# Channel attention and SwiGLU on one core: preparation of the next blocks spread over more steps, its quarter differences on GpSimd

## The chip, the core and the metric

The kernel runs on one core of one Trainium2 chip. A core has TensorE (PE in the profile; PEld is its weight load), VectorE (DVE), ScalarE (ACT), GpSimd (POOL) and SyncE (SP, which here only issues DMAs). Each engine takes its instructions strictly in the order in which the program writes them and waits, where needed, for semaphores of the others. The metric is device time in microseconds (us), lower is better.

## The reference, cut to what matters

```python
def _attn_ref(q, k, v, tau):                    # q, k, v: (2, 6016, 256) float32
    qn = q / (norm(q, axis=1) + 1e-06)
    kn = k / (norm(k, axis=1) + 1e-06)
    s = kn.transpose(0, 2, 1) @ qn / tau        # 256 x 256 per batch
    a = softmax(s)                              # rows
    return v @ a
def _moe_ref(x, w_gate, w_val, w_out, rms_g):   # x: (12032, 256), d_ff = 1536
    xn = x / sqrt(mean(x * x) + 1e-06) * rms_g
    g = xn @ w_gate
    return (silu(g) * (xn @ w_val)) @ w_out
```

## The kernel before, in words

Everything is written out by hand in one order; no scheduler moves anything. Each float32 operand of a matmul is split in a high and a low part (`hi`, `lo`), and each product is made of three matmuls: hi·hi, lo·hi, hi·lo. ScalarE makes the high part with a copy, GpSimd or VectorE subtracts it for the low part.

The tokens are 94 tiles of 128, in 24 blocks: j = 0 to 11 for the first batch, 12 to 23 for the second. A block has four tiles (512 tokens); the last of each batch, 11 and 23, has three (384). A block is worked in NF = 12 steps f, one slice of 128 hidden channels each. Blocks 0 and 1 (`emit_hidden`) use plain products, while the scores of the second batch are made beside block 0. From block 2 on (`j >= WINO`), `emit_step` makes a block's hidden slices with seven half-size products instead of eight, from sums and differences of the four quarters of x (two halves of the channels by two halves of the tokens), called `xp`, and of the weights, called `s`, which `build_s` makes during blocks 1 and 2.

A step from block 2 on has 33 matmuls: 21 for products (7 products of three; 256 columns each, 192 in a three-tile block) and 12 in `emit_out` for the output `po` (three for each tile). Three steps overlap: `now` starts products 5 and 1, `mid` (the step before) adds 3 and 6, `old` (two steps back) adds 7, 2 and 4 and is finished. The products of a step share the PSUM tile `pu`. On PE the order is 7, 2, 5, 1, 3, 6, 4, then the 12 `po`. Product 4 overwrites a half of `pu` that VectorE must have read before (L612, the sum `z = u + t`); so PE's product 4 of each step waits for L612 of that step. VectorE then does L613, and in odd steps L623 and L634 (the multiplication with the Silu of the even step). ScalarE does L619 (copy to `t`), in even steps L621 and L632 (Silu), L628 (the second copy to `t`, which frees the half that product 7 of the next step overwrites), and in odd steps L553 twice (`gh`). GpSimd subtracts L559 twice (`gl`) in odd steps; `emit_out` uses `gh` and `gl` of a step four steps later.

Between the steps stands the preparation of the next block n = j + 1 (`ready`, a table by step; `ready0`, `ready1` and `ready` before, by block). Its pieces are:

- `v_moves`: two 32x32-block transposes of v on VectorE (L366), and the DMA load of a later v. `v_splits`: two ScalarE copies (L349) and two GpSimd subtractions (L350).
- `x(h)`, h = 0 or 1 (two tiles each): 12 matmuls v @ a into the PSUM tile `px` (L386). Before the change all such tiles of later blocks share one bank, tag "m" of `ps_m`.
- `squares_of_x(h)`: ScalarE squares with sums (L402), then two short GpSimd instructions for the inverse root `rr` (L411, L415). `xn(h)`: ScalarE scales `px` by `rr` (L427) into `xn`, which frees `px`.
- `emit_xT_move`: two transposes on VectorE (L463), then 16 DMAs on SP's queue that put the 32x32 blocks in place (`xw` to `xnT`). `xw` and `xp` share one buffer ("moved"), `xn` and `xnT` another ("xn").
- `emit_xT_parts`: ScalarE scales `xnT` by `rms_g` (L485), VectorE makes the differences of quarters `xp` (L490: 512 columns, L495 twice: 256).
- `emit_xT_round(i)`: the hi and lo parts of the quarters and differences in two rounds: two ScalarE copies (L507), two GpSimd subtractions (L509).

`at(j, f, ...)` adds the softmax pieces of the second batch (blocks 4 to 10) and pieces of `build_s` (blocks 1 and 2) behind those of the table.

Of the kernel before, what the change touches and what calls it, by code (L numbers as in the profile page):

```python
# [19 lines left out]
def kernel(  # L20
# [356 lines left out]
    def emit_x(j, h):  # L377
# [3 lines left out]
        psum, tag = (ps_m, "m") if j else (ps_gv, "u")  # L381
# [93 lines left out]

    def emit_xT_parts(j):
# [17 lines left out]
        for o, i0, i1 in ((t2, b2, t1), (t4, a2, t2)):  # L494
            nc.vector.tensor_tensor(out=o, in0=i0, in1=i1, op=ALU.subtract)  # L495
# [96 lines left out]
    def emit_step(j=None, f=None):  # L592
# [31 lines left out]
        if mid:
# [93 lines left out]
    with tc.manual_schedule():  # L718
# [174 lines left out]
        at(6, 7, lambda: softmax_min(1, 1))
        at(7, 7, lambda: (softmax_exp(1, 0), softmax_exp(1, 1)))
        at(B1 - 2, 6, lambda: softmax_div(1, 0))
        at(B1 - 2, 7, lambda: softmax_div(1, 1))
# [5 lines left out]
        def v_moves(n):  # L902
            if n < NB:
                move_v(n, 0)
                move_v(n, 1)
                if 2 < n + 1 < NB:
                    load_v(n + 1)
# [104 lines left out]
```

## Time and profile before

| | us |
|---|---|
| median of 3 runs | 1446.26 (1443.45 to 1446.7) |
| profiled execution | 1446.6 |
| its span | 1444.8 |
| PE busy | 1341.9 (93%) |
| ACT / DVE / POOL busy | 815.9 / 737.9 / 611.5 |
| PE idle before product matmuls L585 with a `w` weight | 68.7 |
| mean granted TensorE clock, share of full | 0.963 |

The busy times say that PE is the engine that works nearly all the time and that each of the others is idle for over four tenths of the span. The time between the span and the device time of the same execution is 1.8 us. Where PE waits, the view of waits names the instruction that released it; the timeline shows what that instruction's engine did before.

### The profile page before, as it was taken

To read this page: it belongs to the slowest core of one execution; us is meant where nothing else is said; L and a number is where in the kernel's file an instruction comes from. 1 tells how busy PE (TensorE), PEld (TensorE's weight loads), DVE (VectorE), ACT (ScalarE), POOL (GpSimd) and SP (SyncE) were. 2 spreads that over 40 slices of the span, in tenths; PEclk is the share of its full clock that TensorE was granted. 3 is DMA by queue.
4 is the path that set the end of the run, shared out by engine and by line. 5 is a ranking of instruction groups with operands and counts; after the bars stand their busy time and mean duration, and the time that the engine had idled before them with its cause. 6 is when DMAs were issued, how large, how long until landed. Compare 5 with 4: busy or idle time off the path is not lost. (4 is left out here: it accounts for less than half of the span.)

```text
span 1444.8 us, 26231 instructions
## 1 busy us (share of the span) xinstructions
PE 1341.9 (93%) x10212; PEld 1295.8 (90%) x10212; DVE 737.9 (51%) x1163; ACT 815.9 (56%) x1727; POOL 611.5 (42%) x550
## 2 busy tenths in 40 slices
PE   7999998899998898999899999999999999999998
PEld 6877887898998898999899898998999999999998
DVE  4689655653544544543543544544544445444443
ACT  4556554565565556555555655565555556555654
POOL 2137444444434444444334444445344434434332
PEclk8999998999999999999999999999999999999999
DMA  8857220120210201101202201201201202101100
GB/s 244 307 177 212 66 44 9 37 44 2 45 38 8 45 15 32 41 12 34 41 9 37 41 23 23 45 12 35 45 7 38 44 4 42 41 1 31 27 16 12
DMA packets 147677, 71.71 MB, mean 50 GB/s; under 512 B 100704, under 2 KB 139104, under 8 KB 147552
## 3 DMA queue, kind: packets, MB, share of 16 engines
q1 hardware_dynamic: 147168, 68.99, 19.2%
q0 software_dynamic: 384, 1.05, 0.4%
q8 instruction: 80, 1.31, 0.4%
q14 instruction: 45, 0.37, 0.1%
HBM read 46.40 MB, written 12.32 MB: 41 GB/s over the span
## 5 line engine op out<-in xcount | busy, mean ns | idle before, releaser
L559 POOL TENSOR_TENSOR gl<-zg,gh 128x512 fp32r<-128x512 f32 (+1 forms) x262 | 328.3, 1275 | 529.9 <-ACT gh L553 334.6
L585 PE MATMUL pu<-xt,w 128*128 128x256 f32 (+1 forms) x2376 | 378.6, 286 | 68.7 <-DVE zg L612 62.7
L619 ACT ACTIVATE t<-pu 128x512 f32<-128x512 f32 (+1 forms) x264 | 155.7, 590 | 486.3 <-DVE zv L613 254.0
L696 PE MATMUL po<-w,gh 128*128 128x256 f32 x2256 | 424.8, 287 | 0.0
L585 PE MATMUL pu<-xt,s 128*128 128x256 f32 (+1 forms) x2376 | 415.2, 284 | 2.1 <-ACT t L628 1.9
L585 PEld LDWEIGHTS pu<-xt,w 128*128 128x128 f32 x2376 | 324.3, 192 | 77.4 <-DVE zg L612 67.3
L696 PEld LDWEIGHTS po<-w,gh 128*128 128x128 f32 x2256 | 359.6, 195 | 2.2 <-ACT gh L553 0.2
L585 PEld LDWEIGHTS pu<-xt,s 128*128 128x128 f32 x2376 | 343.9, 193 | 3.8 <-ACT t L628 3.8
L696 PE MATMUL po<-w,gl 128*128 128x256 f32 x1128 | 322.7, 286 | 0.1
L612 DVE TENSOR_TENSOR zv<-pu,t 128x512 f32<-128x512 f32 (+1 forms) x132 | 88.9, 673 | 361.9 <-issue 184.3
L696 PEld LDWEIGHTS po<-w,gl 128*128 128x128 f32 x1128 | 220.3, 195 | 0.3 <-DVE gl L559 0.3
L553 ACT ACTIVATE gh<-zg 128x512 fp32r<-128x512 f32 (+1 forms) x264 | 157.4, 619 | 25.1 <-DVE zg L623 22.3
L612 DVE TENSOR_TENSOR zg<-pu,t 128x512 f32<-128x512 f32 (+1 forms) x132 | 89.5, 678 | 134.0 <-PE pu L585 93.2
L623 DVE TENSOR_TENSOR zg<-zg,zv 128x768 f32<-128x768 f32 (+1 forms) x132 | 145.8, 1105 | 4.5
L585 PE MATMUL pq<-xt,w 128*128 128x256 f32 (+1 forms) x792 | 139.3, 285 | 0.0
L585 PEld LDWEIGHTS pq<-xt,w 128*128 128x128 f32 x792 | 115.4, 194 | 0.0
L621 ACT ACTIVATE zg<-zg 128x768 f32<-128x768 f32 (+1 forms) x132 | 108.5, 822 | 1.4 <-DVE zg L613 1.4
L174 PE MATMUL s<-raw 128*128 128x256 f32 x376 | 95.2, 412 | 11.3 <-DMA raw<-in_k_dram 11.3
L628 ACT ACTIVATE t<-pu 128x256 f32<-128x256 f32 (+1 forms) x264 | 99.1, 375 | 2.6 <-PE pu L585 0.7
L174 PEld LDWEIGHTS s<-raw 128*128 128x128 f32 x376 | 76.6, 208 | 25.8 <-issue 14.0
L386 PE MATMUL px<-a,vt 128*128 128x256 f32 x564 | 79.1, 290 | 11.9 <-ACT xn L427 11.9
L350 POOL TENSOR_TENSOR vt<-vw,vt 128x512 fp32r<-128x512 f32 (+1 forms) x48 | 64.0, 1353 | 59.7 <-ACT vt L349 59.7
(97 smaller groups left out, 1286.3 us busy)
## 6 DMA issues: line engine op xcount, KB each, us to landing
out_dram<-ob SPq DMA_DIRECT2D x88, 128.0 KB, 2.3
raw<-in_q_dram SPq DMA_DIRECT2D x20, 512.0 KB, 5.8
raw<-in_k_dram SPq DMA_DIRECT2D x20, 512.0 KB, 7.0
v<-in_v_dram SPq DMA_DIRECT2D x80, 128.0 KB, 3.8
xnT<-xw SPq DMA_DIRECT2D x320, 32.0 KB, 1.9
wraw<-in_moe_w_gate_dram SPq DMA_DIRECT2D x12, 256.0 KB, 3.6
wraw<-in_moe_w_val_dram SPq DMA_DIRECT2D x12, 256.0 KB, 4.1
wraw<-in_moe_w_out_dram SPq DMA_DIRECT2D x12, 256.0 KB, 4.7
```

What stands on the lines that cost most here:

```text
L174: nc.tensor.matmul(out=s_ps[b][:, c, :], lhsT=r[:, 1, t, c * P:(c + 1) * P], rhs=r[:, 0, t, :], start=(t0 + t == 0 and c == 0), stop=(t0 + ...
L350: engine.tensor_tensor(out=hl[1], in0=x, in1=f32(hl[0]), op=ALU.subtract)
L386: nc.tensor.matmul(out=px[:, i, :], lhsT=w[:, c, t * P:(t + 1) * P], rhs=x[:, c, :], start=(i == 0 and c == 0 and m == 0), stop=(c == KC - ...
L553: nc.scalar.activation(out=gh, in_=hh, func=AF.Copy)
L559: engine.tensor_tensor(out=gl, in0=hh, in1=f32(gh), op=ALU.subtract)
L585: nc.tensor.matmul(out=out, lhsT=wm[wi], rhs=xm[xi], start=(start and q == 0), stop=(q == 2), skip_group_check=True,)
L612: nc.vector.tensor_tensor(out=z[:, 1:], in0=u, in1=t[:, :2], op=ALU.add)
L619: nc.scalar.activation(out=nt[:, 1:], in_=nu, func=AF.Copy)
L621: nc.scalar.activation(out=zg[:, 1:], in_=zg[:, 1:], func=AF.Silu)
L623: nc.vector.tensor_tensor(out=zg[:, 1:], in0=zg[:, 1:], in1=z, op=ALU.mult)
L628: nc.scalar.activation(out=mt[:, 0], in_=mu[:, 1], func=AF.Copy)
L696: nc.tensor.matmul(out=o_ps[j][t // 2][:, t % 2, :], lhsT=g[:, t * P:(t + 1) * P], rhs=wo[w][:, f, :], start=(first and t % 2 == 0 and m = ...
```

## The change

Seven edits, all in the order of the work and in who does it. The differences of quarters go from VectorE to GpSimd. The scaling by `rms_g` gets a step of its own (`emit_xT_scale`) ahead of them. The second half of `px` and of `pxt` goes to another PSUM bank (`ps_s`) for blocks from 2 on. In `emit_step`, L628 now stands ahead of the Silu (even steps) and of the product of gate and value (odd steps). The table `ready` is written anew: x of a block is made five steps sooner, in the block before the previous one (`then(2, ...)` means block j + 2), with the pieces that depend on each other mostly in different steps; block 2 gets a table of its own. The softmax pieces move to even steps. Two tests `if n < NB` move into `then`.

```diff
-        psum, tag = (ps_m, "m") if j else (ps_gv, "u")
+        psum, tag = (ps_s, "s") if j >= WINO and h else (ps_m, "m") if j else (ps_gv, "u")
         px = psum.tile([P, 2, C], F32, tag=tag, name=f"px_{j}_{h}")
...
+    def emit_xT_scale(j):
+        x = moved[j]
+        for c in range(KC):
+            y = x[:, c, :blocks[j][2] * P]
+            nc.scalar.activation(out=y, in_=y, func=AF.Copy, scale=g_sb[:, c:c + 1])
...
-        for c in range(KC):
-            nc.scalar.activation(
-                out=x[:, c, :2 * h], in_=x[:, c, :2 * h], func=AF.Copy, scale=g_sb[:, c:c + 1]
-            )
-        a1, b1, a2, b2 = (x[:, c, i * h:(i + 1) * h] for c in range(KC) for i in range(2))
-        t1, t2, t3, t4 = (t[:, i, :h] for i in range(4))
-        nc.vector.tensor_tensor(
+        a2, b2 = (x[:, 1, i * h:(i + 1) * h] for i in range(2))
+        nc.gpsimd.tensor_tensor(
             out=t[:, 0:3:2, :h], in0=x[:, :, h:2 * h],
             in1=x[:, 0, :2 * h].rearrange("p (i n) -> p i n", i=2), op=ALU.subtract,
         )
-        for o, i0, i1 in ((t2, b2, t1), (t4, a2, t2)):
-            nc.vector.tensor_tensor(out=o, in0=i0, in1=i1, op=ALU.subtract)
+        for o, i0 in ((1, b2), (3, a2)):
+            nc.gpsimd.tensor_tensor(out=t[:, o, :h], in0=i0, in1=t[:, o - 1 if o == 1 else 1, :h], op=ALU.subtract)
...
-        if old and f % 2 == 0:
-            nc.scalar.activation(out=zg[:, 1:], in_=zg[:, 1:], func=AF.Silu)
-        elif old:
-            nc.vector.tensor_tensor(out=zg[:, 1:], in0=zg[:, 1:], in1=z, op=ALU.mult)
         if mid:
             _, _, _, mproduct, mu, mt = mid
             mproduct(3, mu[:, 0])
             mproduct(6, mu[:, 1])
             nc.scalar.activation(out=mt[:, 0], in_=mu[:, 1], func=AF.Copy)
+        if old and f % 2 == 0:
+            nc.scalar.activation(out=zg[:, 1:], in_=zg[:, 1:], func=AF.Silu)
+        elif old:
+            nc.vector.tensor_tensor(out=zg[:, 1:], in0=zg[:, 1:], in1=z, op=ALU.mult)
...
-        at(5, 7, lambda: softmax_min(1, 0))
+        at(5, 4, lambda: softmax_min(1, 0))
...
+        def then(m, *go):
+            def run(n):
+                for g in go if n + m - 1 < NB else ():
+                    g(n + m - 1)
+            return run
+
+        def both(n):
+            emit_xT_parts(n)
+            emit_xT_round(n, 0)
+
+        def rest(n):
+            emit_xT_round(n, 1)
+
+        steady = {
+            2: then(2, v_moves),
+            3: then(2, v_splits),
+            7: then(2, x(0)),
+            8: then(2, x(1), squares_of_x(0)),
+            9: then(2, xn(0)),
+            10: then(2, squares_of_x(1)),
+            11: then(2, xn(1)),
+        }
         ready = {
-            0: (xn(0), x(1)),
-            1: (squares_of_x(1),),
-            2: (xn(1), emit_xT_move),
-            4: (lambda n: v_moves(n + 1),),
-            6: (lambda n: v_splits(n + 1),),
-            7: (emit_xT_parts,),
-            8: (lambda n: emit_xT_round(n, 0),),
-            9: (lambda n: emit_xT_round(n, 1),),
-            10: (lambda n: n + 1 < NB and x(0)(n + 1),),
-            11: (lambda n: n + 1 < NB and squares_of_x(0)(n + 1),),
+            **{f: (go,) for f, go in steady.items()},
+            0: (emit_xT_move,),
+            4: (emit_xT_scale,),
+            5: (both,),
+            7: (rest, steady[7]),
         }
+        ready2 = {
+            **ready,
+            0: (xn(1),),
+            1: (emit_xT_move,),
+            4: (),
+            5: (emit_xT_scale,),
+            6: (both,),
+        }
         ready1 = {
...
+            0: (x(0), squares_of_x(0)),
+            1: (xn(0),),
+            2: (x(1), squares_of_x(1)),
+            3: (xn(1),),
+            4: (emit_xT_move,),
+            5: (then(2, v_moves),),
+            6: (then(2, v_splits),),
+            8: (emit_xT_scale, lambda n: both(n), then(2, x(0))),
+            9: (then(2, x(1)),),
+            10: (rest, then(2, squares_of_x(0)),),
+            11: (then(2, xn(0), squares_of_x(1)),),
         }
```

The first place is VectorE in steps 5 to 7 of block 12, where block 13 is prepared. Before, between the products of an odd step and the sum L612 of the next:

```order
L613 TENSOR_TENSOR zv_5_8915<-pq_5_8911,t_5_8807 128x256
L623 TENSOR_TENSOR zg_4_8866<-zg_4_8866,zv_5_8915 128x768
L634 TENSOR_TENSOR zg_4_8866<-pu_5_8806,zg_4_8866 128x256
L490 TENSOR_TENSOR xp_8959<-xnT_8681 128x2x256
L495 TENSOR_TENSOR xp_8959<-xnT_8681,xp_8959 128x256 x2
L612 TENSOR_TENSOR zg_6_8974<-pu_6_8857,t_6_8858 128x512
```

The same place of the changed kernel, where the line numbers are a little higher (L612 is L613, L623 is L629):

```order
L614 TENSOR_TENSOR zv_5_8915<-pq_5_8923,t_5_8815 128x256
L629 TENSOR_TENSOR zg_4_8884<-zg_4_8884,zv_5_8927 128x768
L635 TENSOR_TENSOR zg_4_8884<-pu_5_8814,zg_4_8884 128x256
L613 TENSOR_TENSOR zg_6_8995<-pu_6_8875,t_6_8876 128x512
L614 TENSOR_TENSOR zg_6_8995<-pq_6_8991,t_6_8876 128x256
```

The three subtractions of quarters are gone from VectorE. The second place is GpSimd in the same block. Before, behind the pair `gl` of step 5 (hidden slices 2 and 3):

```order
L559 TENSOR_TENSOR gl_3_8840<-zg_2_8762,gh_3_8839 128x512
L350 TENSOR_TENSOR vt_14_8901<-vw_8798,vt_14_8900 128x512 x2
L559 TENSOR_TENSOR gl_4_8938<-zg_4_8866,gh_4_8937 128x512
L559 TENSOR_TENSOR gl_5_8940<-zg_4_8866,gh_5_8939 128x512
L509 TENSOR_TENSOR xt_13_8958<-xnT_8681,xt_13_8957 128x256
L509 TENSOR_TENSOR xt_13_8958<-xnT_8681,xt_13_8957 128x512
L559 TENSOR_TENSOR gl_6_9044<-zg_6_8974,gh_6_9043 128x512
```

The same place of the changed kernel:

```order
L560 TENSOR_TENSOR gl_3_8848<-zg_2_8776,gh_3_8847 128x512
L491 TENSOR_TENSOR xp_8867<-xnT_8593 128x2x256
L496 TENSOR_TENSOR xp_8867<-xnT_8593,xp_8867 128x256 x2
L510 TENSOR_TENSOR xt_13_8866<-xnT_8593,xt_13_8865 128x256
L510 TENSOR_TENSOR xt_13_8866<-xnT_8593,xt_13_8865 128x512
L560 TENSOR_TENSOR gl_4_8950<-zg_4_8884,gh_4_8949 128x512
L560 TENSOR_TENSOR gl_5_8952<-zg_4_8884,gh_5_8951 128x512
L510 TENSOR_TENSOR xt_13_8866<-xp_8867,xt_13_8865 128x512 x2
L411 TENSOR_SCALAR ss_0_9043<-ss_0_9043 128x2
```

The three subtractions and the first round now stand between two pairs `gl`, and the v subtractions L350 have moved ahead of them. The third place is ScalarE at the start of block 2, where the seven-product steps begin (`t_0` is the copy that product 3 waits for). Before:

```order
L553 ACTIVATE gh_11_1882<-zh_11_1876 128x512
L402 ACTIVATE xn_1898,ss_0_1899<-px_0_1849 128x256 x2
L619 ACTIVATE t_0_1906<-pu_0_1905 128x512
L427 ACTIVATE xn_1898<-px_0_1849,rr_0_1903 128x256 x2
L619 ACTIVATE t_1_1934<-pu_1_1933 128x512
L628 ACTIVATE t_0_1906<-pu_0_1905 128x256
L402 ACTIVATE xn_1898,ss_1_1949<-px_1_1916 128x256 x2
```

The same place of the changed kernel:

```order
L554 ACTIVATE gh_11_1902<-zh_11_1896 128x512
L427 ACTIVATE xn_1875<-px_0_1769,rr_0_1880 128x256 x2
L402 ACTIVATE xn_1875,ss_1_1920<-px_1_1819 128x256 x2
L620 ACTIVATE t_0_1927<-pu_0_1926 128x512
L427 ACTIVATE xn_1875<-px_1_1819,rr_1_1924 128x256 x2
L620 ACTIVATE t_1_1942<-pu_1_1941 128x512
L625 ACTIVATE t_0_1927<-pu_0_1926 128x256
```

The scaling of the first half and the squares of the second now stand ahead of the first copy `t_0`, and `px` has left the steps of block 2's start.

## Rows read from the trace of the kernel before

**Rows 1.** Windows: length, busy (instructions) of PE, PEld, DVE, ACT, POOL, granted clock, DMA.

```profile
234.00:1445.00 1211.00, 1127.29 (x9134) 1112.15 (x9132) 573.86 (x977) 690.74 (x1523) 509.66 (x468) 0.97 0.14 28
```

**Rows 2.** Timeline of PE, 806 to 824 us: start, duration, instruction [idle before <- releaser].

```profile
806.22 0.51 PE L585 MATMUL pu<-xt,s 128*128 128x256 f32 x3
...
817.91 0.51 PE L585 MATMUL pu<-xt,s 128*128 128x256 f32 x3
...
819.69 0.51 PE L585 MATMUL pu<-xt,s 128*128 128x256 f32 x3
823.19 0.62 PE L585 MATMUL pu<-xt,w 128*128 128x256 f32 x3 [2.99 <-DVE zg L612]
```

**Rows 3.** PE's waits from 234 to 1445 us: total us, times, longest us.

```profile
PE pu L585 <- DVE zg L612: 62.7, 23, 3.9
PE px L386 <- ACT xn L427: 7.9, 20, 0.4
PE pu L585 <- DVE zv L612: 5.9, 20, 1.8
PE pu L585 <- ACT t L628: 1.9, 2, 1.4
```

**Rows 4.** Timeline of DVE, 806 to 823.5 us.

```profile
807.88 0.96 DVE L623 TENSOR_TENSOR zg<-zg,zv 128x768 f32<-128x768 f32 x1
...
815.68 2.07 DVE L623 TENSOR_TENSOR zg<-zg,zv 128x768 f32<-128x768 f32 x1
...
820.19 1.42 DVE L490 TENSOR_TENSOR xp<-xnT 128x512 f32<-128x512 f32 x1 [2.11 <-ACT xnT L485]
821.65 0.89 DVE L495 TENSOR_TENSOR xp<-xnT,xp 128x256 f32<-128x256 f32 x2
```

**Rows 5.** Timeline of PE, 877 to 884 us.

```profile
877.43 1.01 PE L585 MATMUL pu<-xt,w 128*128 128x256 f32 x3 [2.99 <-DVE zg L612]
...
883.76 0.51 PE L585 MATMUL pu<-xt,s 128*128 128x256 f32 x3
```

**Rows 6.** Windows of PE alone, from 870 to 880 us: busy, granted clock, DMA.

```profile
870.00:880.00 10.00, 7.01 (x50) 0.83 0.17 27
```

**Rows 7.** Timeline of PE, the start of block 2.

```profile
228.21 0.51 PE L585 MATMUL pu<-xt,s 128*128 128x256 f32 x3
...
232.20 2.93 PE L386 MATMUL px<-a,vt 128*128 128x256 f32 x12 [3.13 <-ACT xn L427]
...
243.46 0.62 PE L585 MATMUL pu<-xt,s 128*128 128x256 f32 x3
```

**Rows 8.** Timeline of PE, block 23's steps and the last matmul.

```profile
1428.28 0.48 PE L585 MATMUL pu<-xt,s 128*128 128x192 f32 x3
...
1431.68 0.48 PE L585 MATMUL pu<-xt,s 128*128 128x192 f32 x3
...
1439.67 0.28 PE L696 MATMUL po<-w,gl 128*128 128x256 f32 x1
```

**Rows 9.** Timeline of POOL, 806 to 832 us.

```profile
814.38 2.54 POOL L350 TENSOR_TENSOR vt<-vw,vt 128x512 fp32r<-128x512 f32 x2 [2.25 <-ACT vt L349]
...
825.84 1.99 POOL L509 TENSOR_TENSOR xt<-xnT,xt 128x256 fp32r<-128x256 f32 x2 [4.78 <-ACT xt L507]
```

**Rows 10.** Timeline of ACT, 803 to 824 us.

```profile
808.87 1.26 ACT L553 ACTIVATE gh<-zg 128x512 fp32r<-128x512 f32 x2
...
813.66 1.16 ACT L349 ACTIVATE vt<-vw 128x512 fp32r<-128x512 f32 x2
...
818.83 1.32 ACT L485 ACTIVATE xnT<-xnT,g_sb 128x512 f32<-128x512 f32 x2
```

**Rows 11.** Timeline of DVE at the start of block 2.

```profile
244.52 1.31 DVE L463 STREAM_TRANSPOSE xw<-xn 128x512 f32<-128x512 f32 x2 [2.83 <-ACT xn L427]
```

**Rows 12.** Timeline of SP's DMA queue, 800 to 816 us.

```profile
800.31 11.09 SPq L470 DMA_DIRECT2D xnT<-xw  x16
```

**Rows 13.** Timeline of ACT at the start of block 2.

```profile
231.31 0.84 ACT L427 ACTIVATE xn<-px,rr 128x256 f32<-128x256 f32 x2 [1.61 <-POOL rr L415]
```

More of the change, by code (lines that the diff above doesn't have):

```diff
@@ L447, in emit_xT_first @@
             if c == 0 or j == 0:
-                psum, tag = (ps_m, "m") if j else (ps_gv, "u")
+                psum, tag = (ps_s, "s") if j >= WINO and h else (ps_m, "m") if j else (ps_gv, "u")
                 ps = psum.tile([P, KC, 2, P], F32, tag=tag, name=f"pxt_{j}_{h}_{c}")
@@ L888 @@
             at(2, i // 2, go)
-        at(4, 6, lambda: inverse_norms(1))
-        at(4, 7, lambda: spread_norms(1, ps_m, "m"))
-        at(4, 8, lambda: keep_norms(1))
-        at(5, 7, lambda: softmax_min(1, 0))
[L893 to L896, printed above, removed]
+        at(4, 2, lambda: inverse_norms(1))
+        at(4, 3, lambda: spread_norms(1, ps_m, "m"))
+        at(4, 4, lambda: keep_norms(1))
+        at(5, 4, lambda: softmax_min(1, 0))
+        at(6, 4, lambda: softmax_min(1, 1))
+        at(7, 6, lambda: (softmax_exp(1, 0), softmax_exp(1, 1)))
+        at(B1 - 2, 4, lambda: softmax_div(1, 0))
+        at(B1 - 2, 6, lambda: softmax_div(1, 1))
         steps = [(j, f) for j in range(NB) for f in range(NF)]
@@ L902, in v_moves @@
         def v_moves(n):
[L903 to L907, printed above, removed]
+            move_v(n, 0)
+            move_v(n, 1)
+            if 2 < n + 1 < NB:
+                load_v(n + 1)
         def v_splits(n):
-            if n < NB:
-                for c in range(KC):
-                    split_v(n, c, nc.gpsimd)
+            for c in range(KC):
+                split_v(n, c, nc.gpsimd)
         def x(h):
@@ L934 @@
+        ready2 = {
[5 more added lines that the diff above has]
+            6: (both,),
         }
         ready1 = {
-            0: (x(0),),
-            1: (squares_of_x(0),),
-            2: (xn(0), x(1)),
-            3: (squares_of_x(1),),
-            4: (xn(1), emit_xT_move),
-            5: (lambda n: v_moves(n + 1),),
-            6: (lambda n: v_splits(n + 1),),
-            8: (emit_xT_parts,),
@@ L944 @@
-            9: (lambda n: emit_xT_round(n, 0),),
-            10: (lambda n: emit_xT_round(n, 1), lambda n: x(0)(n + 1)),
-            11: (lambda n: squares_of_x(0)(n + 1),),
+            0: (x(0), squares_of_x(0)),
[7 more added lines that the diff above has]
+            9: (then(2, x(1)),),
@@ L972 @@
             if n < NB:
-                for go in (ready0, ready1, ready)[min(j, 2)].get(f, ()):
+                for go in (ready0, ready1, ready2, ready)[min(j, 3)].get(f, ()):
                     go(n)
```

## The prediction

> **What bounds the kernel now.** I read the windows by stage first, then PE's waits in the long stage, then the timeline around one wait on each engine, and last the start of that stage. From 234 us on PE is busy for 1127.3 of 1211 us, and no other engine for more than 690.7 [rows 1]. So PE sets the end, and the question is what PE loses. The reader is to see four things.
>
> Without a wait a step is quick: three steps lie between 806.22 and 817.91, so one takes 3.90 us and each of its 33 matmuls 0.118 [rows 2].
>
> PE's waits come to 62.7 + 7.9 + 5.9 + 1.9 = 78.4 us, and nearly all of it is one wait a block: product 4 for VectorE's sum L612, 23 times [rows 3]. In the block shown it lasts 2.99 us [rows 2], because VectorE first makes the quarter differences, L490 and L495, and these wait for ScalarE's scaling [rows 4]. So a chain ScalarE, VectorE, ScalarE stands in VectorE's queue ahead of a sum that PE needs. The two smaller waits are of the same kind: `px` of the second half waits until `xn` has emptied the one bank (20 times, 0.4 at most), and L612 of step 1 waits behind the transposes, which wait for `xn` of the same step.
>
> A wait costs more than it lasts. The matmuls on both sides of the 2.99 us start 3.50 apart where 0.35 would do [rows 2], so 3.15 are lost. And the clock falls behind it: after another 2.99 us without a matmul, the next 30 take from 877.43 to 883.76, 6.33 us [rows 5], where 30 times 0.118 are 3.54; the granted clock of 870 to 880 is 0.83 [rows 6], a mixture of its levels 2.4 and 1.2 GHz. Over the stage it is 0.97 [rows 1]: 3% of 1211, some 36 us.
>
> The block that starts the stage is rough: from 228.21 to 243.46 three short steps take 15.25 us [rows 7].
>
> **The whole loss, from a count.** From the first seven-product matmul at 228.21 [rows 7] to the end of the last matmul, 1439.67 + 0.28 [rows 8], are 1211.7 us. In it lie 22 blocks x 12 steps x 21 = 5544 product matmuls (504 of them, in blocks 11 and 23, with 192 columns), 86 tiles x 36 plus 24 left from block 1 = 3120 for `po`, and 480 for `px`. A 192-column step takes 1431.68 - 1428.28 = 3.40 [rows 8]; less nine `po` at 0.118 that is 0.111 for one product. With 11.69 / 99 = 0.1181 unrounded, 8640 x 0.1181 + 504 x 0.111 = 1076.3. So PE loses 1211.7 - 1076.3 = 135 us here: 78.4 of waits [rows 3], 3.1 of `px` at 232 [rows 7], some 36 of clock, and the rest, about 17, is what refilling after some 65 waits takes beyond the idle time shown (0.16 to 0.3 each).
>
> **The change part by part.** All sums are against the profiled execution's own 1446.6 (span 1444.8 and 1.8 around it); the median of the runs is 0.3 lower.
>
> *Differences to GpSimd, scaling a step earlier.* VectorE loses 1.42 + 0.89 = 2.3 us a block [rows 4] and, more, the wait for ScalarE. L612 of the next even step then finds VectorE free. The place that is late next would be GpSimd. A subtraction with 512 columns takes 2.54 / 2 = 1.27 there, a pair of 256 and 512 takes 1.99, so 256 takes 0.72 [rows 9]; the three differences are not in the trace, and by these rows cost 1.27 + 2 x 0.72 = 2.7 (bounds: 2.3 at VectorE's price, 5.8 at the factor 2.07 / 0.96 that VectorE's L623 shows while L350 runs [rows 4, 9]; L350 itself was not slowed by that collision, so I take 2.7). In a clean odd step `gh` starts 2.65 after the step's start and lasts 1.26 [rows 2, 10], so the `gl` pair runs from about 3.3 to 5.9, that is until 2.0 into the next step. Behind the pair of step 5 stand now 2.7 of differences and 1.99 of round 0: GpSimd is free 2.8 into step 7, and the next `gl` pair wants it at 3.3 (or later, where L629 is slowed). Behind that pair comes round 1, 2.5, until 4.5 into step 8, while steps 7 and 8 have grown by a half `px` each, 12 x 0.118 = 1.4. So it fits once a block with half a microsecond to spare, and each later use has more: the first `gl` is ready 4.6 after an odd step's start and is read by PE at 3.90 + 23 x 0.118 = 6.6. Round 1 is needed only at the next block, four steps later.
>
> *L629 beside GpSimd.* In step 7 L629 now runs while GpSimd subtracts, as L623 did at 815.68: 2.07 instead of 0.96 [rows 4]. That makes `gh` 1.1 late, out of the 2.0 of slack; no PE wait.
>
> The Trainium skill speaks against this edit: "GPSIMD Engine Reference" (4.1 Engine selection) says that two-input elementwise work belongs on VectorE, GpSimd being about half as fast, and its key points say that the two share SBUF interfaces. The trace agrees: 1.27 for 512 columns against VectorE's 0.96 for 768, and the 2.07. What the rule makes of the time is the first rival below.
>
> *x five steps sooner, one piece a step; the second bank.* VectorE's transposes L463 start in step 0 when `xn` is over since step 11, so the zv waits go; in an even step VectorE has done its two sums after some 1.66 us (where L623 starts in an odd one [rows 2, 4]) and is next asked for behind product 2 of the next step, 3.90 + 0.6; of these 2.8 us the two transposes use 1.31 [rows 11]. The `px` waits go with the bank. The 16 DMAs, 11.1 us [rows 12], follow the transposes in step 0 at 1.66 + 1.31 and are issued by 14.1; the scaling comes after step 4, at 5 x 3.90 = 19.5. That is four steps where there were five, with 5.4 us to spare. ScalarE is fullest after step 3: `gh` from 2.65 for 1.26, two copies of `po` (512 columns each, no longer than that pair) and L349 1.16 [rows 10] end by 6.3, 2.4 into step 4, where L620 asks at about 1.7, behind VectorE's sums. That is 0.7 late at most; PE asks for this copy at product 3 of step 5, 2.8 us later. The scaling, 1.32 [rows 10], comes behind that step's Silu, two microseconds before the next L620.
>
> *L628 ahead of the Silu.* It holds PE only at two places of the old kernel (1.9 us [rows 3]); it delays the Silu by 0.3, which has slack. Nothing.
>
> *Softmax pieces on even steps.* The longest waits, up to 3.9 [rows 3], lose what they had above 2.99; that is in the sum already.
>
> *Start of block 2.* The 3.1 us of `px` at 232 go, but a new wait comes: ScalarE must scale the first half and square the second before copy `t_0`, and that scaling waits for `rr`, which on GpSimd stands behind round 1 of block 2. Before, the same wait for `rr` held ScalarE 1.61 us [rows 13] and PE 3.13 [rows 7]. Of the 15.25 us there, 51 products and `po` and 12 `px` are work, 63 x 0.118 = 7.4; 7.8 are lost. I take 7 for after, bounds 3 (only the copies' own latency) and 10. The pieces of `build_s` that crowd VectorE in block 2 stay: 3, bounds 0 and 6. For the 21 other blocks together 3 (0 to 10, half a microsecond each).
>
> **Sum.** 1446.6 - 135 - 1 (the same `px` wait in block 1, between 0 and the 3.1 of the one at 232) + 7 + 3 + 3 = 1323.6, rounded to 1324. The bounds, 3 and 26 in place of the 13, give 1314 to 1337 (two less or one more by the wait in block 1).
>
> **The rivals.** *GpSimd is late, by little.* If two-input work on both engines slows both, the differences take up to 5.8 instead of 2.7; less the half microsecond to spare, the `gl` pair of step 7 is then 2.6 us late, with L629's 1.1 up to 3.7, against 2.0 of slack and the 1.4 of a half `px`. PE would wait 0.3 to 1.7 in each of 21 blocks, say 1, short beside the 2.99 behind which the clock fell; with a refill of 0.3 that is 1.3 x 21 = 27: 1351. For it: GpSimd is filled without a gap from step 5 to step 8. Against it: L350's unslowed 2.54 in just such a collision [rows 4, 9].
>
> *Half the gain.* One wait of about 3 us a block remains, at another place (the scaling for the 16 DMAs, say), with refill and clock as now, (62.7 x 3.15 / 2.99 + 36) = 102 of the 135 kept: 1426. Against it: the 5.4 us to spare.
>
> *Slower.* ScalarE takes its queue in order, and `xn` waits in it for `rr`. `rr` is now behind the differences, two rounds and two pairs on GpSimd. If it comes later than ScalarE wants it, L620 and L625 of the next step stand behind `xn`, and PE stops for products 3 and 7. The start of block 2 gives the price: 3.13 of PE, and then 12 `px` in 2.93 us [rows 7] instead of 1.4 and slow matmuls behind, together about 6. Once in each of 21 blocks that is 126: 1450. It decides when `rr` is more than 2.6 us late (it should be ready 1.3 into step 9, and ScalarE asks for it at 3.9).
>
> *It does nothing.* Some hidden order keeps L612 behind; the DVE order speaks against it, as nothing stands between L635 and L613 there.
>
> **How the numbers follow.** Forecast 0.73, with a range of its own from 1314 to 1337; GpSimd a little late 0.17; half the gain 0.05; slower 0.03; nothing 0.02. The range reaches from 1312 to 1360, which takes in most of the first rival. What this kernel's measurement can tell from no change is 0.2%, 3 us; faster 0.95, same 0.02, slower 0.03.
>
> **What would show it.** Right: PE's waits for L613 nearly gone outside block 2; `px` without a wait; a granted clock of 0.99 or more in the stage; a block of four tiles in 49.6 us (12 x 3.90 and 24 x 0.118) instead of about 55; L629 at two microseconds once a block; the start of block 2 with PE waiting for `t` L620 or L625. Wrong: waits of PE for `gl`, ScalarE waiting for `rr` in every block, or a clock that falls although PE works on.

## The result and the profile after

The changed kernel takes 1325.84 us (median of 4 runs, 1324.72 to 1328.8) against 1446.48 of the kernel before beside it (1443.45 to 1446.73): a ratio of 0.9174, with a 95% interval from 0.9153 to 0.9194. The forecast was 1324. The profiled execution took 1328.8, its span is 1326.7, and the mean granted clock rose from 0.963 to 0.990. Some line numbers have moved: the sum L612 is L613, L585 is L586, L619 is L620, L628 is L625, L623 is L629, L634 is L635, L490 and L495 are L491 and L496, L509 is L510, L559 is L560, L485 is L480.

PE's waits from the start of the seven-product stage to the end (total us, times, longest), which answer to [rows 3]:

```profile
PE pu L586 <- DVE zg L613: 6.0, 2, 3.7
PE pu L586 <- ACT t L620: 2.9, 1, 2.9
PE pu L586 <- ACT t L625: 1.3, 1, 1.3
PE pu L586 <- DVE zv L613: 0.9, 2, 0.5
```

78.4 us have become 11.1 (counted from 228 us, where [rows 3] begins at 234), and the 23 waits for the sum of an even step are two. The windows (length, busy of PE, PEld, DVE, ACT, POOL, granted clock, DMA), which answer to [rows 1], say where the rest is:

```profile
228.00:245.00 17.00, 12.85 (x93) 12.43 (x93) 13.77 (x22) 9.94 (x25) 5.84 (x7) 0.90 0.11 26
245.00:290.00 45.00, 38.46 (x294) 37.67 (x293) 28.65 (x40) 25.78 (x60) 24.30 (x23) 0.92 0.12 27
290.00:1326.00 1036.00, 1031.33 (x8756) 1030.49 (x8754) 481.80 (x859) 665.15 (x1444) 551.45 (x507) 1.00 0.15 31
```

From 290 us on nothing is lost but some 1.3 us in the last steps, and the granted clock is 1.00. All else that is left lies in block 2, from 228 to 289 us. GpSimd's timeline shows one block of the even stretch and the same place of the next (start, duration, instruction, count, idle before):

```profile
754.66 1.29 POOL L491 TENSOR_TENSOR xp<-xnT 128x512 f32<-128x512 f32 x1
756.02 1.55 POOL L496 TENSOR_TENSOR xp<-xnT,xp 128x256 f32<-128x256 f32 x2
757.53 2.78 POOL L510 TENSOR_TENSOR xt<-xnT,xt 128x256 fp32r<-128x256 f32 x2
760.28 2.54 POOL L560 TENSOR_TENSOR gl<-zg,gh 128x512 fp32r<-128x512 f32 x2
762.78 2.54 POOL L510 TENSOR_TENSOR xt<-xp,xt 128x512 fp32r<-128x512 f32 x2
...
804.25 1.32 POOL L491 TENSOR_TENSOR xp<-xnT 128x512 f32<-128x512 f32 x1
```

Two readings. A block lasts 804.25 - 754.66 = 49.59 us, where the prediction counted 49.6 for a block without a loss. And the differences take 1.29 + 1.55 = 2.84 (2.7 were estimated); GpSimd then works without a gap from 754.66 to 765.3. VectorE beside it, in step 7 and at the start of step 8 (the same columns), which answers to [rows 4], with PE at the start of step 7:

```profile
757.07 0.69 DVE L613 TENSOR_TENSOR zv<-pu,t 128x512 f32<-128x512 f32 x1 [2.83 <-ACT zg L633]
...
758.20 0.96 DVE L629 TENSOR_TENSOR zg<-zg,zv 128x768 f32<-128x768 f32 x1
...
762.43 0.69 DVE L613 TENSOR_TENSOR zg<-pu,t 128x512 f32<-128x512 f32 x1 [2.79 <-PE pu L586]
```

```profile
756.46 0.51 PE L586 MATMUL pu<-xt,s 128*128 128x256 f32 x3
```

The sum L613 of the even step now waits for PE alone: VectorE has been idle for 2.79 us ahead of it, where before it had the differences and ScalarE's scaling in front of it. Step 7 starts at 756.46 on PE, so L629 begins 1.7 us into it, and takes 0.96, not the 2.07 that was expected.

The stage can be compared between kernels without the loading at the start, which differs by some microseconds from one execution to the next: from the first seven-product matmul to the start of the last `po`. Before the change 1076.0 us of it are work. The changed kernels make the second half of block 3's `px` ahead of the stage, so that 468 of the 480 `px` matmuls are left in it, and have 12 x 0.118 less, 1074.6. The profiled executions:

| kernel | first, last (us) | stage | lost |
|---|---|---|---|
| before | 228.21, 1439.67 | 1211.5 | 135.5 |
| changed | 228.40, 1321.54 | 1093.1 | 18.5 |
| changed, differences on VectorE | 228.88, 1351.91 | 1123.0 | 48.4 |
| before, differences on GpSimd | 227.40, 1351.55 | 1124.2 | 48.2 |
| before, second `px` bank | 228.32, 1421.82 | 1193.5 | 117.5 |
| changed, copy behind the Silu | 228.26, 1321.82 | 1093.6 | 19.0 |
| changed, differences twice | 224.97, 1317.31 | 1092.3 | 17.7 |
| changed, one wait a block put back | 230.23, 1377.24 | 1147.0 | 72.4 |
| changed, `build_s` spread | 225.94, 1311.25 | 1085.3 | 10.7 |
| changed, first mended start | 230.41, 1315.02 | 1084.6 | 10.0 |
| changed, both mended | 230.49, 1310.50 | 1080.0 | 5.4 |

### The profile page after: what moved, and what is told of

Its sections match the earlier page's. It is cut to its first block, busy times and chain, and to the rows that moved or that the text cites. A ratio compares the mean times of both kernels' runs of the same rounds, so it can differ in the third digit from the quotient of the medians.

```text
span 1326.7 us, 26330 instructions
## 1 busy us (share of the span) xinstructions
PE 1292.4 (97%) x10212; PEld 1260.7 (95%) x10212; DVE 686.3 (52%) x1097; ACT 824.3 (62%) x1727; POOL 681.7 (51%) x616
## 3 DMA queue, kind: packets, MB, share of 16 engines
q8 instruction: 80, 1.31, 0.4%
## 4 chain that ended last, share of the span: by engine, by line
PE 79%; DVE 0%; ACT 0%; issue 0%; ACTq 0%; DVEq 0%
PE pu L586 41%; PE po L697 27%; PE pq L586 7%; PE px L386 4%; DVE w L544 0%; DVE zg L629 0%; ACT zg L627 0%; DVE zg L613 0%; ACT ob L708 0%; DVE gl L560 0%; DVE zv L613 0%; ACT gh L554 0%; PE pq L258 0%; ACTq L1031 0%; DVE zv L614 0%
## 5 line engine op out<-in xcount | busy, mean ns | idle before, releaser
L560 POOL TENSOR_TENSOR gl<-zg,gh 128x512 fp32r<-128x512 f32 (+1 forms) x262 | 327.9, 1272 | 425.0 <-ACT gh L554 227.4
L697 PE MATMUL po<-w,gh 128*128 128x256 f32 x2256 | 411.5, 281 | 0.0
L586 PE MATMUL pu<-xt,s 128*128 128x256 f32 (+1 forms) x2376 | 407.6, 280 | 1.3 <-ACT t L625 1.3
L620 ACT ACTIVATE t<-pu 128x512 f32<-128x512 f32 (+1 forms) x264 | 155.4, 589 | 376.6 <-DVE zv L614 201.8
L586 PE MATMUL pu<-xt,w 128*128 128x256 f32 (+1 forms) x2376 | 370.8, 282 | 9.8 <-DVE zg L613 6.0
L697 PEld LDWEIGHTS po<-w,gh 128*128 128x128 f32 x2256 | 349.0, 190 | 2.2 <-ACT gh L554 0.2
L586 PEld LDWEIGHTS pu<-xt,s 128*128 128x128 f32 x2376 | 336.5, 189 | 1.5 <-ACT t L625 1.5
L586 PEld LDWEIGHTS pu<-xt,w 128*128 128x128 f32 x2376 | 320.6, 189 | 11.0 <-DVE zg L613 6.6
L697 PE MATMUL po<-w,gl 128*128 128x256 f32 x1128 | 316.1, 280 | 0.1
L613 DVE TENSOR_TENSOR zv<-pu,t 128x512 f32<-128x512 f32 (+1 forms) x132 | 89.7, 680 | 336.6 <-ACT zg L633 144.3
L697 PEld LDWEIGHTS po<-w,gl 128*128 128x128 f32 x1128 | 213.5, 189 | 0.3 <-DVE gl L560 0.3
L613 DVE TENSOR_TENSOR zg<-pu,t 128x512 f32<-128x512 f32 (+1 forms) x132 | 89.7, 680 | 197.2 <-PE pu L586 192.0
L586 PE MATMUL pq<-xt,w 128*128 128x256 f32 (+1 forms) x792 | 136.1, 281 | 0.0
L629 DVE TENSOR_TENSOR zg<-zg,zv 128x768 f32<-128x768 f32 (+1 forms) x132 | 125.6, 951 | 14.0 <-DVE zv L614 0.5
L586 PEld LDWEIGHTS pq<-xt,w 128*128 128x128 f32 x792 | 111.8, 189 | 0.0
L625 ACT ACTIVATE t<-pu 128x256 f32<-128x256 f32 (+1 forms) x264 | 100.0, 379 | 4.3 <-PE pu L586 1.7
L198 DVE TENSOR_TENSOR acc<-acc,sq 128x1024 f32<-128x1024 f32 (+1 forms) x47 | 65.4, 1392 | 30.1 <-ACT sq L189 27.8
L386 PE MATMUL px<-a,vt 128*128 128x256 f32 x564 | 75.3, 283 | 0.0
```

The lines of the kernel that those rows point to most:

```text
L198: engine.tensor_tensor(out=a, in0=a, in1=sq, op=ALU.add)
L386: nc.tensor.matmul(out=px[:, i, :], lhsT=w[:, c, t * P:(t + 1) * P], rhs=x[:, c, :], start=(i == 0 and c == 0 and m == 0), stop=(c == KC - ...
L560: engine.tensor_tensor(out=gl, in0=hh, in1=f32(gh), op=ALU.subtract)
L586: nc.tensor.matmul(out=out, lhsT=wm[wi], rhs=xm[xi], start=(start and q == 0), stop=(q == 2), skip_group_check=True,)
L613: nc.vector.tensor_tensor(out=z[:, 1:], in0=u, in1=t[:, :2], op=ALU.add)
L620: nc.scalar.activation(out=nt[:, 1:], in_=nu, func=AF.Copy)
```

## The experiments

**The two halves of the edit, each alone.** First the changed kernel with the differences back on VectorE, so that everything but the move to GpSimd is kept:

```diff
-        nc.gpsimd.tensor_tensor(
+        nc.vector.tensor_tensor(
...
-            nc.gpsimd.tensor_tensor(out=t[:, o, :h], in0=i0, in1=t[:, o - 1 if o == 1 else 1, :h], op=ALU.subtract)
+            nc.vector.tensor_tensor(out=t[:, o, :h], in0=i0, in1=t[:, o - 1 if o == 1 else 1, :h], op=ALU.subtract)
```

> The changed kernel with the three quarter differences back on VectorE, at the same place of the program (step 5, behind the second product of the gate, L635), everything else as changed. It tells whether the move to GpSimd or the earlier scaling took the wait for L613 away. My theory: both did, mostly the earlier scaling. L635 ends 3.2 us into an odd step of 3.90, the differences take 2.3 (rows 4), so they end 1.6 into the next step, L613 takes 0.69 and ends at 2.3, where product 4 asks at 2.13; where a pair `gl` of GpSimd lies beside the differences, they come up to 1.3 later. That is 0.2 to 1.5 us of PE waits in each of 22 blocks, 5 to 30 us, and the clock stays at 0.99 or more because no wait is near 3 us: 1331 to 1356. Rival: VectorE's queue is the whole matter, the wait of about 3 us a block comes back and the clock with it: 62.7 to 100 us more, 1390 to 1426.

Measured: 1358.41 us (1355.36 to 1359.6), 0.9391 of before [0.9377, 0.9406]; just above my range, far below the rival's. One of the 20 waits for L613 outside block 2, on VectorE:

```profile
816.76 0.42 DVE L635 TENSOR_TENSOR zg<-pu,zg 128x256 f32<-128x256 f32 x1
817.19 0.69 DVE L491 TENSOR_TENSOR xp<-xnT 128x512 f32<-128x512 f32 x1
817.92 2.82 DVE L496 TENSOR_TENSOR xp<-xnT,xp 128x256 f32<-128x256 f32 x2
820.66 0.68 DVE L613 TENSOR_TENSOR zg<-pu,t 128x512 f32<-128x512 f32 x1
```

on GpSimd at the same time, and on PE:

```profile
817.49 2.97 POOL L560 TENSOR_TENSOR gl<-zg,gh 128x512 fp32r<-128x512 f32 x2 [2.72 <-issue]
```

```profile
821.39 0.62 PE L586 MATMUL pu<-xt,w 128*128 128x256 f32 x3 [1.21 <-DVE zg L613]
```

L491 needs only 0.69 when it comes first. [rows 4] had it at 1.42, at 820.19, while GpSimd was in this pair:

```profile
818.54 2.53 POOL L559 TENSOR_TENSOR gl<-zg,gh 128x512 fp32r<-128x512 f32 x2 [1.62 <-issue]
```

So even before the change half of it was waiting for GpSimd. The two L496 then take 2.82, not 0.89, behind the pair `gl`. PE waits 0.95 to 1.31 us in each of those 20 blocks, and the granted clock stays at 1.00 from 290 to 1320 us. With x made sooner and the scaling a step earlier, ScalarE's part of the wait is gone (L491 starts right behind L635); the collision with GpSimd keeps 1.2 of its 3 us. No run takes the earlier scaling apart from the earlier x.

Then the kernel before with nothing but the differences on GpSimd:

```diff
-        nc.vector.tensor_tensor(
+        nc.gpsimd.tensor_tensor(
...
-            nc.vector.tensor_tensor(out=o, in0=i0, in1=i1, op=ALU.subtract)
+            nc.gpsimd.tensor_tensor(out=o, in0=i0, in1=i1, op=ALU.subtract)
```

> The kernel before with one edit: the three quarter differences on GpSimd instead of VectorE, at the old place (step 7, behind ScalarE's scaling). My theory: the sum L612 no longer stands behind them, so the 62.7 us of waits for it (rows 3) and their refill (x 3.15 / 2.99 = 66) go, and the clock's 36 us; the waits for px (7.9) and zv (5.9) and the start of block 2 stay. 1446 - 102 = about 1345, between 1340 and 1365. Rival: the order of x and v is what counts, and with the scaling still in step 7 the chain only comes late on GpSimd (rounds needed at the next block's start): a wait for xt at each block's start, 1400 or more.

Measured: 1357.85 us (1356.91 to 1358.48), 0.939 [0.9377, 0.9403], inside the range. PE's waits in the stage:

```profile
PE px L386 <- ACT xn L427: 11.3, 21, 3.5
PE pu L585 <- DVE zv L612: 5.8, 20, 1.8
PE pu L585 <- DVE zg L612: 5.4, 4, 3.7
PE pu L585 <- ACT t L628: 4.0, 2, 3.6
```

The 62.7 us have gone to 5.4 by this edit alone, and the short waits that it doesn't touch are left, as expected. So each half alone brings 88 of the 120 us. The 56 us that either would bring (88 + 88 - 120) are most of the 3 us wait and its clock. Some 32 us are left to the other half: here the short waits for `px` and zv, there the 20 waits that the collision with GpSimd leaves.

**The second `px` bank alone, and the copy behind the Silu.**

```diff
-        psum, tag = (ps_m, "m") if j else (ps_gv, "u")
+        psum, tag = (ps_s, "s") if j >= WINO and h else (ps_m, "m") if j else (ps_gv, "u")
```

> The kernel before with one edit: the second half of px (and of the transposed x) in a bank of its own. My theory: the 7.9 us of waits for xn L427 (rows 3) go with 20 refills of 0.16 to 0.3, and the 3.1 at 232 us (rows 7) goes in part: 11 to 16 us less, 1431 to 1435. Rival: the wait is hidden anyway, since PE then reaches the wait for L612 sooner and waits longer there: no change, 1443 to 1447.

Measured: 1428.32 us (1427.09 to 1429.51), 0.9878 [0.9864, 0.9891]: 17.4 less, a little more than expected. The wait for `px` is gone, and the wait that the rival would have had grow stays at 62.4:

```profile
PE pu L585 <- DVE zg L612: 62.4, 23, 3.9
PE pu L585 <- DVE zv L612: 5.9, 20, 1.8
PE pu L585 <- ACT t L628: 1.8, 2, 1.1
```

The undone order of L625:

```diff
+        if old and f % 2 == 0:
+            nc.scalar.activation(out=zg[:, 1:], in_=zg[:, 1:], func=AF.Silu)
+        elif old:
+            nc.vector.tensor_tensor(out=zg[:, 1:], in0=zg[:, 1:], in1=z, op=ALU.mult)
         if mid:
...
-        if old and f % 2 == 0:
-            nc.scalar.activation(out=zg[:, 1:], in_=zg[:, 1:], func=AF.Silu)
-        elif old:
-            nc.vector.tensor_tensor(out=zg[:, 1:], in0=zg[:, 1:], in1=z, op=ALU.mult)
```

> The changed kernel with one edit undone: the copy of product 6 (L625) behind the Silu and the gate's first product again, as before the change. My theory: it costs nothing, PE waits for L625 nowhere outside block 2: 1326 within 3 us (1323 to 1329). Rival: with VectorE and ScalarE unblocked the copy is the next to be late; product 7 of the next step waits 0.2 to 0.5 us in some hundred steps: 1345 or more.

Measured: 1327.26 us (1325.48 to 1329.15), 0.9178 [0.9164, 0.9191] where the changed kernel has 0.9174. This edit gives nothing that can be measured.

**What a wait costs.** VectorE is made late once a block by ten more transposes, which only write over a tile that is written again later:

```diff
+        def hold(n):
+            if n + 2 < NB:
+                nn = blocks[n + 2][2]
+                for i in range(10):
+                    nc.vector.transpose(
+                        out=by_tile(v_w[n + 1][:, i % 2], nn),
+                        in_=v_t[n + 2][:, :A * nn, i % 2, :].rearrange("p (a t) r -> p a t r", a=A),
+                    )
+
+        ready[6] = (hold,)
```

> The changed kernel with ten more transposes on VectorE in step 6 of blocks 3 to 20 (18 blocks; they only write over a tile that is written again later), 10 x 0.65 = 6.5 us, so that one sum L613 per block is late and PE waits some 2.8 us for it; GpSimd, ScalarE and the order of everything else stay as changed. It tells what one wait a block costs apart from its length. My theory, as in the prediction: each wait costs its length, 0.16 to 0.3 of refill, and the granted clock falls behind it as it did before the change (0.97 over the stage, 36 us for 23 waits, 28 for 18): 1326 + 18 x 2.8 + 4 + 28 = about 1408, clock 0.96 to 0.98. Rival: a wait costs its length and the refill only, and the clock before was low for another cause: 1326 + 50 + 4 = about 1380, clock 0.99.

Measured: 1383.28 us (1378.73 to 1384.16), 0.9542 [0.9512, 0.9571]. The waits came out shorter than I had worked out: 20 of 37.2 us in all, 14 of them of 2.07. The time lies near the rival's 1380, but the rival counted 50 us of waits and a clock of 0.99, and here the clock is 0.974 in the profiled execution. So neither sum fits as written, and the answer lies in the single waits. Two of equal length, on PE:

```profile
430.09 0.62 PE L586 MATMUL pu<-xt,w 128*128 128x256 f32 x3 [2.07 <-DVE zv L613]
...
482.02 0.62 PE L586 MATMUL pu<-xt,w 128*128 128x256 f32 x3 [2.07 <-DVE zv L613]
```

and the 8 us behind each (length, busy and matmuls of PE, granted clock, DMA):

```profile
430.09:438.09 8.00, 8.00 (x67) 1.00 0.00 0
482.02:490.02 8.00, 8.00 (x54) 0.79 0.01 2
```

Behind the first the clock stays at 2.4 GHz. Behind the second it is a mixture with 1.2 GHz, and 13 matmuls fewer are done, 13 x 0.118 = 1.5 us. Of the 14 waits of 2.07 us six look like the second and eight like the first; the two longer ones (2.33 and 3.59) fell too. A block with a wait but no fall lasts 482.02 - 430.09 = 51.93, so the wait cost 51.93 - 49.59 - 2.07 = 0.27 beyond its length. Together 37.2 - 0.9 more idle time than in the changed kernel, 18 x 0.27 = 5 of refill and 8 x 1.5 to 1.7 = 13 of clock make 54. The medians differ by 57, the stages of the two profiled executions by 1147.0 - 1093.1 = 53.9. My theory's terms are there, but a fall is not certain after a wait of this length, and its length alone doesn't tell which one is followed by a fall. The kernel before shows the same behind waits of 2.99 us:

```profile
1212.24:1220.24 8.00, 7.97 (x65) 1.00 0.00 0
1266.49:1274.49 8.00, 8.00 (x44) 0.62 0.00 0
```

Of its 20 waits over 1.5 us behind block 2, 5 had no fall in the 8 us after them, 11 a clock of 0.79 to 0.82 there, and 4 one of 0.62 to 0.65: 11 x 8 x 0.2 + 4 x 8 x 0.37 = 29 us, most of the 36 that the prediction set down.

**GpSimd's slack.**

```diff
+        for _ in range(2 if j > WINO else 1):
             nc.gpsimd.tensor_tensor(
...
```

> The changed kernel with the three quarter differences done twice on GpSimd for the blocks from 3 on (the same values written again), 2.8 us more of GpSimd in steps 5 and 6 of 21 blocks. It measures the slack that the prediction's likeliest rival doubted. My theory: the pair `gl` of step 7 is then ready 2.8 later than its 5.1 after the step's start, and PE reads it 8.0 after the start because a half px lies in steps 7 and 8: 0 to 0.5 us of waits a block, 1326 to 1337. Rival: GpSimd is nearly full there, each further microsecond on it reaches PE: 1 to 2 us in 21 blocks and refills, 1351 to 1375.

Measured: 1328.61 us (1324.63 to 1329.62), 0.9166 [0.9138, 0.9193]: no change. With 2.8 us more on GpSimd PE's only wait from 290 us to the end is one of 0.4 in the last block:

```profile
PE pu L587 <- DVE zv L614: 0.4, 1, 0.4
```

So GpSimd can be 2.8 us later before PE notices, and hardly more. In the changed kernel the first `gl` of the pair at 760.28 is ready at about 761.6, and PE first reads it at 764.52; in this run (ready at 760.0, read at 760.27) about 0.3 of these 2.9 us are left.

**Block 2.** PE at its start, in the changed kernel:

```profile
228.40 0.51 PE L586 MATMUL pu<-xt,s 128*128 128x256 f32 x3
...
232.87 0.62 PE L586 MATMUL pu<-xt,w 128*128 128x256 f32 x3 [2.89 <-ACT t L620]
...
235.12 0.99 PE L586 MATMUL pu<-xt,s 128*128 128x256 f32 x3 [1.27 <-ACT t L625]
...
240.66 0.52 PE L586 MATMUL pu<-xt,s 128*128 128x256 f32 x3
...
272.54 0.87 PE L586 MATMUL pu<-xt,w 128*128 128x256 f32 x3 [3.72 <-DVE zg L613]
```

ScalarE ahead of the first copy, which answers to [rows 13], and VectorE ahead of the longest wait:

```profile
230.76 0.84 ACT L427 ACTIVATE xn<-px,rr 128x256 f32<-128x256 f32 x2 [2.14 <-POOL rr L415]
...
232.20 0.61 ACT L620 ACTIVATE t<-pu 128x512 f32<-128x512 f32 x1
```

```profile
268.01 2.47 DVE L544 TENSOR_TENSOR s<-wk,s 128x512 fp32r<-128x512 f32 x2 [2.44 <-ACT s L541]
270.40 1.48 DVE L544 TENSOR_TENSOR w<-wk,w 128x256 fp32r<-128x256 f32 x1
271.81 0.68 DVE L613 TENSOR_TENSOR zg<-pu,t 128x512 f32<-128x512 f32 x1
```

Two causes, then: ScalarE waits for `rr` with the copy `t_0` behind it, and the pieces of `build_s` (L544 here) stand ahead of L613 and wait for ScalarE and, while GpSimd does a round, for GpSimd. I first mended both at once:

```diff
-            weights[1, f] = [pieces.pop(0) for _ in range(2)]
-        for i, go in enumerate(pieces):
-            at(2, i // 2, go)
+            weights[1, f] = [pieces.pop(0) for _ in range(3)]
+        for f, go in zip((4, 4, 6, 6, 7, 8), pieces):
+            at(2, f, go)
...
         ready2 = {
             **ready,
-            0: (xn(1),),
-            1: (emit_xT_move,),
-            4: (),
+            0: (xn(0),),
+            1: (squares_of_x(1), xn(1)),
+            2: (emit_xT_move,),
+            3: (then(2, v_moves),),
+            4: (then(2, v_splits),),
...
-            11: (then(2, xn(0), squares_of_x(1)),),
```

> The changed kernel with block 2's start mended: in block 1 three pieces of build_s a step instead of two (30 of 36; the last six spread over steps 4 to 8 of block 2 in place of two a step from step 0), and block 3's scaling xn moved from step 11 of block 1 and step 0 of block 2 to steps 0 and 1 of block 2, with its transposes, 16 DMAs and the moves of v each one step later. My theory: the changed kernel still loses 11 us of PE's idle time between 230 and 275 us and some 5 by the clock there (0.90 to 0.92); without ScalarE waiting for rr ahead of the copies and without the pieces of build_s beside GpSimd's subtractions most of it goes: 1311 to 1316. Rival: block 1's VectorE and GpSimd are then full and PE loses it there, or block 3's x comes late behind the later DMAs: 1324 to 1332.

Measured: 1319.7 us (1318.23 to 1322.09), 0.9108 [0.9081, 0.9134]: half of what I expected, and the stage still loses 10.0 us. VectorE worked at the pieces beyond the end of block 1, where the stage began at 230.41:

```profile
228.45 4.72 DVE L537 TENSOR_TENSOR wk<-wk 128x256 f32<-128x256 f32 x4
233.09 0.68 DVE L679 TENSOR_TENSOR zh<-zh,pv 128x512 f32<-128x512 f32 x1
```

So block 1's last hidden state (L679) came late, and ScalarE's `gh` of it, with `t_0` behind, waited for it until 233.80. The next two have no piece in the last step of block 1, and L679 starts 0.4 us after the stage does. First the pieces alone, with block 3's `xn` as changed:

```diff
-            weights[1, f] = [pieces.pop(0) for _ in range(2)]
-        for i, go in enumerate(pieces):
-            at(2, i // 2, go)
+            weights[1, f] = [pieces.pop(0) for _ in range(3 if f < 11 else 0)]
+        for f, go in zip((2, 2, 4, 4, 4, 5, 6, 8, 8), pieces):
+            at(2, f, go)
```

> The changed kernel with one edit in block 2's start: build_s has 27 of its 36 pieces in steps 2 to 10 of block 1 (three a step, none in step 11), and the other nine in steps 2 to 8 of block 2 instead of two a step from step 0; xn of block 3 stays as changed. It separates the two causes that the run on the start of block 2 mended together (it came out 6 us below the changed kernel, with VectorE full until 233 us in block 1). My theory: the longer waits of block 2 (L613, 2.3 and 3.7 us, and the clock behind them) were build_s standing on VectorE ahead of L613 and held up by GpSimd's subtractions; they go, 6 to 9 us: 1317 to 1320. ScalarE's wait for rr (2.9 us at L620) stays. Rival: the waits come from ScalarE behind rr, and the pieces only follow: 1323 to 1329.

Measured: 1321.68 us (1318.21 to 1322.42), 0.912 [0.9099, 0.9142]; the median lies between the two ranges, but it holds the loading at the start. The stage tells them apart: 7.8 us less than the changed kernel's, the 6 to 9 of my theory, and what is left of PE's waits is ScalarE's, with its clock, and three short ones:

```profile
PE pu L586 <- ACT t L620: 2.9, 1, 2.9
PE pu L586 <- ACT t L625: 1.2, 1, 1.2
PE pu L586 <- DVE zv L613: 0.8, 2, 0.5
PE pu L586 <- POOL xt L510: 0.8, 1, 0.8
```

Then this distribution together with the `ready2` of the first mended start, of which it changes only this:

```diff
-            weights[1, f] = [pieces.pop(0) for _ in range(3)]
-        for f, go in zip((4, 4, 6, 6, 7, 8), pieces):
+            weights[1, f] = [pieces.pop(0) for _ in range(3 if f < 11 else 0)]
+        for f, go in zip((2, 2, 4, 4, 4, 5, 6, 8, 8), pieces):
```

> The same distribution of build_s together with block 3's xn in steps 0 and 1 of block 2 (and its transposes, 16 DMAs and the moves of v a step later). Compared with the first version of the mended start it leaves VectorE free in the last step of block 1, so that the hidden state of that step comes on time and ScalarE reaches the first copy t_0 without waiting. My theory: of the 4.7 us of PE's waits that were left there 3 go, and the clock of 0.80 in 228 to 245 us rises to 0.9 or more, 2 us: 1313 to 1317. Rival: the first copies of the stage are late by their own latency (PE asks for t_0 before ScalarE can have copied it), and nothing more is to be had: 1317 to 1321.

Measured: 1314.17 us (1312.26 to 1317.45), 0.9074 [0.9052, 0.9095], in the range. It beats both kernels. PE's waits from 222 us on, and the windows:

```profile
PE pu L586 <- ACT t L625: 1.5, 1, 1.5
PE pu L586 <- POOL xt L510: 0.8, 1, 0.8
PE pu L586 <- DVE zv L613: 0.4, 1, 0.4
```

```profile
228.00:245.00 17.00, 14.71 (x113) 13.69 (x112) 10.49 (x18) 12.79 (x33) 8.33 (x9) 1.00 0.06 14
245.00:290.00 45.00, 45.00 (x381) 44.83 (x381) 27.63 (x47) 30.56 (x68) 27.54 (x25) 1.00 0.20 40
```

The wait for `t_0` and the fall of the clock behind it are gone. Of the stage's 18.5 us of loss `build_s` had 7.8, ScalarE's `xn` ahead of the copies another 5.3, and 5.4 remain, 3.6 of them in block 2.

## Why the prediction was right, point by point

**The whole loss of 135 us and the 49.6 a block** held: the even stretch runs at exactly that, so nearly everything above the count of matmuls was loss that could go, and the new order loses 0.3 of it in 21 blocks (3 were set down). Some 1.3 us in the last steps were there before and stay.

**The chain ScalarE, VectorE, ScalarE ahead of the sum** was the cause. Of the two halves of the edit, the move to GpSimd alone takes the 3 us wait away, and the rest alone cuts it to 1.2. The prediction put both into one term and did not say that either would do for most of it.

**The clock.** 36 us were read from a granted clock of 0.97. Counted over the 8 us behind each wait it is about 29 behind block 2 and some 7 in it. The 29 went with the waits; in block 2 some 5 are left (a granted clock of 0.79 to 0.81 in the 8 us behind the waits at 232.87, 249.19 and 272.54).

**GpSimd.** The price of the differences was right (2.84 for 2.7). The place where they fit was right, by a wrong account. L629 was to take 2.07 and make `gh` late; instead it takes 0.96, and the second L510 beside it about 0.8 longer (2.78 a pair for 1.99). GpSimd is free 3.85 into step 7 (760.31 - 756.46), where 2.8 were worked out, so the half microsecond to spare was overrun. PE did not notice, because more slack stands behind it: the prediction had 2.0 and a half `px` of 1.4, the rows show 2.9. The first rival fails by its premise: the differences took 2.84, not up to 5.8. The factor 2.07 / 0.96 behind the 5.8 was a wait for one instruction of GpSimd, not a price by size. Had they taken 3 us more, as the rival has it, the run with the differences twice shows that the slack would just have been used up.

**L625 ahead of the Silu: nothing**, and nothing it was. **The `px` bank**: 7.9 of waits, their 20 refills (0.16 to 0.3 each) and 3.1 at 232 stand in the 135, some 14 to 17 together. Alone it gave 17.4: 5 at block 2's start (product 7 of its third step begins at 233.09, where before it began at 238.16), and 12 that the 7.9 and the refills account for. The 1 us for a `px` wait in block 1 was right: one of 0.9 was there, and it is gone. The softmax pieces were not tried apart.

**The start of block 2**: 7 set down. The first three steps take 240.66 - 228.40 = 12.26 for 51 matmuls, 6.0 of work, so 6.2 are lost, and the longest wait there is the one foretold (`t` L620 behind `rr`).

**The pieces of `build_s`: 3, bounds 0 and 6.** This term failed. Block 2 lost 16.7 us (372 matmuls from 228.40 to 289.06), nearly as much as the 19.2 before the change: 6.2 in its first three steps and 10.5 behind them. With the pieces spread, 0.8 of the 10.5 are left; its first three steps then lost 8.1, at a granted clock of 0.76 for 0.86, so that the stage gained 7.8. I had carried the 3 over from the waits of before, and not seen that GpSimd's differences and rounds of block 3 come into the same steps as the pieces.

The sum of the terms, 13, was 5.5 short of the 18.5 that the stage still loses. This term was 7.5 short and the 1.3 in the last steps stood in no term, while the 21 other blocks lost 2.7 less than their 3 and the start 0.8 less than its 7. The profiled execution, the slowest of the four, is 5 above the forecast. That the median is only 2 above it is in part luck: errors of either sign met, and the executions differ by 4.

## What to carry to other kernels

Count the matmuls of a stage, take the step time of a clean stretch, and what lies above the product is the loss to look for; here it was 135, and all but 18.5 of it went. Here the wait that stood once a block on the bounding engine went when the work in front of it moved to another engine, and shrank from 3 us to 1.2, behind which the clock did not fall, when that work's operand came earlier; test each half alone before doing both. What is carried over from a stage that waited (here 3 us for the pieces of `build_s`) has to be worked out anew against what now runs in the same steps. Before two-input elementwise work goes from VectorE to GpSimd, look at what VectorE reads from SBUF with both operands at that moment, and at the engine that starts later.

## What the runs showed of the hardware

**VectorE and GpSimd exclude each other, instruction by instruction.** Where both operands of VectorE's instruction lie in SBUF and GpSimd subtracts beside it, the one that starts first keeps its time and the other takes longer. GpSimd first: L623 2.07 for 0.96 [rows 4], L496 2.82 for 0.89, the single L544 at 270.40 1.48 for the 0.42 that it takes undisturbed. VectorE first: GpSimd's pair L510 2.78 for 1.99 beside an L629 of 0.96, and the pair `gl` 2.97 for 2.54 beside an L491 of 0.69 and an L496. L613, with one operand in PSUM, takes 0.69 whatever GpSimd does (757.07 in the rows above, and all 229 of this size from 290 to 1320 us in the changed kernel). The Trainium skill says this in "SBUF — State Buffer" (SBUF: two separate sides; Who interferes with whom): a VectorE instruction with two SBUF inputs contends with a GpSimd instruction that reads SBUF, and the pair of ports is a lock, not a shared bandwidth. These rows agree with it. The prediction's sum had taken VectorE to be the one that is held up.

**Equal waits, unequal falls.** Behind idle times of 2.07 us on PE, in otherwise dense work, the granted clock fell in 6 of 14 cases (the run with one wait a block put back), behind 0.95 to 1.31 us in none of 20 (the run with the differences on VectorE), and behind 1.63 to 3.89 us in 15 of 20 (the kernel before, behind block 2).
